# Chunked retention and a two-layer feed-forward on one core: a merged visit, a split last visit, held stores, and constants built by GpSimd

## The chip, the cores and the metric

The kernel runs on one core of one Trainium2 chip. The metric is the device time of one execution in microseconds (us). All times in this document are in us unless marked ns. The engines are called TensorE (PE in the profile, PEld for its weight loads), VectorE (DVE), ScalarE (ACT), GpSimd (POOL) and SyncE (SP); SPq and ACTq are the queues on which SP and ACT issue DMAs.

## The reference

Inputs q, k, v have shape (4, 8, 768, 64): 4 batches, 8 heads, 768 tokens, 64 features, float32. A decaying state runs over the tokens of each batch and head, and its output goes, heads joined, through two matrices with a leaky rectifier between them (w_in 512 x 2048, w_out 2048 x 512, alpha 2048).

```python
gamma = 1.0 - 2.0 ** (-5.0 - np.arange(H))
for t in range(S):
    state = gamma * state + outer(k[t], v[t])       # per batch and head, 64 x 64
    y[t] = q[t] @ state / sqrt(D)
x = y.transpose(0, 2, 1, 3).reshape(B * S, H * D)   # 3072 x 512
h = x @ w_in
out = (np.maximum(h, 0) + alpha * np.minimum(h, 0)) @ w_out   # 3072 x 512, float32
```

## The kernel before, in words

**Tiling.** The recurrence is computed in chunks. A unit u is 256 tokens of one batch (12 units); it has two windows w = 2u and 2u + 1 (24 windows). Up to window 7 a window is four heads of all 256 tokens, from window 8 on it is all heads of 128 tokens. Within a chunk the work is products of 64x64 tiles, four of which lie in PE's array at a time: scores (sc, keys with queries), a mask by DVE, products of the masked scores with v and of the queries with the carried state (both into y), and sums of keys with v for the next state. k and q are scaled beforehand by powers of gamma from a small table `tab` (kdq, by GpSimd or DVE), so the carried state tg needs a product with a power of gamma only now and then. ACT copies a finished y into xT, the input of the feed-forward.

The feed-forward works on blocks n = 0 to 5 of 512 tokens (two units each). `ffn1(n)` multiplies xT with w_in (hps), ACT makes the negative part (hm) and DVE joins both into gt; `ffn2(n)` multiplies gt with w_out (ops), ACT empties each finished bank into an os tile, and SP stores it. In `ffn2` each group of 128 tokens takes 16 products of 512 columns into one bank; block 0 takes three groups side by side (banks fa, fb, pa) and then the fourth (fa again).

**Order.** All order is written out by hand; each engine takes its instructions in the order of the program. `ffn1` and `ffn2` are generators, and `tick(gen, m)` lets m of their products go. Between ticks the program puts visits to the recurrence. A visit `both(u_old, u_new)` (L567 to L694) lets an old unit leave (products within the chunks L609, carries of state L587, ACT's copy to xT L660) and a new one enter (scores L632, sums L646, mask L669, states L681 to L687); either may be missing. The carries come in two halves, chunk equal to row half and unequal; the second half writes the same banks from the other row half and waits for `through(...)`, a tiny ACT instruction that tells that the first is done. Where no unit enters, three products of `gen` (`mid`, L622) fill that wait.

For n from 1 to 4 the loop at the end (L938 to L961) runs `ffn1(n)` and `ffn2(n)` with the visits for block n + 1, whose units are u0 = 2(n + 1) and u0 + 1: in block 1 `both(None, 4)`, `both(4, 5)`, `both(5, None)`; in block 2 `both(None, 6)`, `both(6, 7)`, `both(7, 8)`; later `both(u0, u0 + 1)` and `both(u0 + 1, u0 + 2)`, and in block 4 `both(11, None)` at the end. The first units go by functions of their own (`scores`, `within`, `finish`, `enter`, `pass_on`), with products of ones (`busy`) between them in the opening. `ahead()` scales the next window's k and q on GpSimd, has SP issue a DMA that transposes them into kq (`prep`, L233), and has SP load the window two further on (`load`, L169).

**Queues and buffers.** Nearly all DMAs are issued by SP, in the program's order: loads of q, k, v (L161, L169), of the weights in pieces (`fetch`, L192), the transposes and the stores (L797). q, k, v and the weight pieces share three rings of eight buffers (`ks`, `qs`, `vs`); stores have six of their own (`os`). A table `tab` (48 KB), a constant `mi` with mask and identity (128 KB) and alpha are loaded by ACT's queue first (L810 to L812).

Of the kernel before, what the change touches and what calls it, by code (L numbers as in the profile page):

```python
# [18 lines left out]
def kernel(  # L19
# [32 lines left out]
    pos = np.arange(128) % 64  # L52
    for a in range(2):
        for g in range(2):
            for x in range(2):
                for r in range(2):
                    h = 4 * g + 2 * r + x
                    col = 8 * g + 4 * r + 2 * x + a
                    tab_np[:, col] = g64[h] ** (127.0 - (2 * pos + a))
                    tab_np[:, 16 + col] = scale * g64[h] ** (2 * pos + a + 1.0 - 128.0)  # L60
    for g in range(2):
        for x in range(2):
            for r in range(2):
                tab_np[64 * r : 64 * r + 64, 32 + 2 * g + x] = g64[4 * g + 2 * r + x] ** 128
    for h in range(H):
        tab_np[:, 64 + h] = g64[h] ** (127.0 - np.arange(128))
        tab_np[:, 72 + h] = scale * g64[h] ** (np.arange(128) + 1.0 - 128.0)
# [3 lines left out]
    mi_np = np.zeros((128, 512), dtype=np.float16)  # L71
    for a in range(2):
        for b in range(2):
            mi_np[:, 128 * a + 64 * b : 128 * a + 64 * b + 64] = (2 * pos + a)[:, None] <= (
                2 * np.arange(64) + b
            )[None, :]
    mi_np[:, 256:384] = np.eye(128)
    mi_np[:, 384:448] = pos[:, None] <= np.arange(64)[None, :]

    tab_h = nc.inline_tensor(tab_np, name="tab_const")  # L80
    mi_h = nc.inline_tensor(mi_np, name="mi_const")
# [265 lines left out]
    def state(w, cs=None):  # L347
        u, g, b, c3 = place(w)
        decay = tab[:, 32 + 2 * g : 34 + 2 * g].unsqueeze(2).to_broadcast([128, 2, D])
        for c in cs or chunks(w):  # L350
            stv = sums.pop((w, c))[:, 0:128].rearrange("p (x e) -> p x e", e=D)
            gs = slice(2 * g, 2 * g + 2)
            if c3 + c > 0:
                nc.vector.tensor_tensor(out=stv, in0=tgs[2 * u + c][:, gs], in1=stv, op=ADD)
            to = 2 * u + c + 1 if 2 * u + c + 1 < NPE else 2 * NPE
            if to not in tgs:
                tgs[to] = new_state()
            nc.vector.tensor_tensor(out=tgs[to][:, gs], in0=stv, in1=decay, op=MULT)
# [130 lines left out]
    def all_state(key, cols):  # L489
        stv = cols.rearrange("p (z e) -> p z e", e=D)  # L490
        if key % (2 * NUS):
            nc.vector.tensor_tensor(out=stv, in0=tgs[key], in1=stv, op=ADD)
        to = key + 1 if key + 1 < NPE else 2 * NPE
        tgs[to] = new_state()
        nc.vector.tensor_tensor(
            out=tgs[to], in0=stv, in1=tab[:, 32:36].unsqueeze(2).to_broadcast([128, 4, D]), op=MULT
        )
# [69 lines left out]
    def both(u_old, u_new, mid=None):  # L567
# [11 lines left out]
        def carry(w, y, same, after=None):  # L579
            u, t, b, c3 = place(w)  # L580
            kq = live[w][1]
            for z in range(4):
                for r in range(2):
                    c = r if same else 1 - r
                    if c3 + 2 * t + c == 0:
# [5 lines left out]
                        start=False,  # L591
                        stop=True,
                        skip_group_check=True,
                    )
                    if after is not None:
# [4 lines left out]
        if old:  # L600
# [19 lines left out]
            done = through(last, nc.scalar)  # L620
            if not new:
                mid()  # L622
# [30 lines left out]
        if old:  # L653
            for w in old:
                carry(w, y, False, done if w == old[0] else None)
                live.pop(w)
            n, i = divmod(u_old, 2)
            if i == 0:
                xT[n] = new_x(n)
            nc.scalar.activation(  # L660
                out=xT[n][:, 4 * i : 4 * i + 4].rearrange("p s r (c i) -> p (s r) c i", c=2),
                in_=y.rearrange("p (c s i) -> p s c i", c=2, i=64),
                func=COPY,
                bias=0.0,
                scale=1.0,
            )
# [98 lines left out]
    def ffn2(n, groups=((0,), (1,), (2,), (3,)), tags="ffff", split=()):  # L765
# [3 lines left out]
        for tqs in groups:  # L769
# [3 lines left out]
            for at in parts:  # L773
                m = at.stop - at.start
                opss = {tq: ps("ops", tags[tq])[:, 0:m] for tq in tqs}
                for ft, tq in ((ft, tq) for ft in range(NFT) for tq in tqs):
# [7 lines left out]
                    if ft == NFT - 1:  # L784
                        row = TB * n + 128 * tq
                        for e in range(2 if at.start else 1):
                            cut = slice(e * m // 2, (e + 1) * m // 2) if at.start else slice(0, m)
                            os_sb = sbp.tile([128, d_model], FP, tag="os", bufs=6, name="os")
# [5 lines left out]
                            else:  # L794
                                nc.vector.tensor_copy(out=os_sb, in_=opss[tq][:, cut])  # L795
                            cols = slice(at.start + cut.start, at.start + cut.stop)
                            (nc.scalar if at.start and e == 0 else nc.sync).dma_start(  # L797
                                out=out[row : row + 128, cols], in_=os_sb
# [10 lines left out]
    nc.vector.memset(ones, 1.0)  # L809
    nc.scalar.dma_start(out=tab, in_=tab_h.ap())  # L810
    nc.scalar.dma_start(out=mi, in_=mi_h.ap())
# [67 lines left out]
    for i in range(4):  # L879
        if i == 1:  # L880
            load(5, "kq")
        for j in range(4):
            fetch("wo", i, j)
        if i < 2:
            load(4 + i, "v")
# [14 lines left out]
    gen = ffn2(0, ((0, 1, 2), (3,)), ("fa", "fb", "pa", "fa"))  # L900
# [7 lines left out]
    prep(7, opening=True)  # L908
# [29 lines left out]
    for n in range(1, NBLK):  # L938
# [9 lines left out]
        if n + 1 < NBLK:  # L948
            early = n < 3
# [3 lines left out]
            ahead()  # L953
            ahead()
# [3 lines left out]
            more_units = n > 1 and 2 * u0 + 4 < NW  # L958
            both(u0 + 1, u0 + 2 if more_units else None, lambda: tick(gen, 3))
# [32 lines left out]
```

## Time and profile before

| | before |
|---|---|
| time, median of 3 runs (lowest to highest) | 207.14 (206.74 to 207.25) |
| profiled execution, its own time | 205.89 |
| profiled execution, span from first to last instruction | 204.1 |
| granted TensorE clock, mean | 1.00 |
| PE / DVE / ACT / POOL busy | 197.7 / 122.0 / 98.0 / 76.7 |
| read from HBM, written to it | 27.45 MB, 6.29 MB |

The profile is of one execution. Its page gives busy times, the span in 40 slices, and the chain of work that ended last; the trace behind it answers with the chain piece by piece, the timeline of an engine, groups of instructions by line, and waits. L and a number is a line of the kernel before, except where a view of the kernel after is shown. A PE that is busy isn't a PE at its peak, and spans on POOL are rough.

### The profile page before, as it was taken

The page shows a single profiled execution, that of the slowest core. Times are in us where ns is not written, and L with a number is a line of the kernel's source. Part 1 is how long each engine was busy: PE and PEld are TensorE (multiplying, and loading weights), DVE is VectorE, ACT ScalarE, POOL GpSimd, SP SyncE. Part 2 cuts the span into 40 slices and gives each one's busy share as a digit, 9 for nine tenths or more (in the row PEclk, how much of TensorE's full clock was granted, in tenths as well). Part 3 has the DMA queues.
Part 4 walks back from the last instruction along what each step waited for, and adds up shares of the span by engine and source line. Part 5 has one row for each costly group of instructions (what it writes and reads, how often), then busy time and mean ns, then how long its engine had stood idle before and what let it go on. Part 6 is the DMA issues. An engine that isn't in the chain of part 4 may idle for free.

```text
span 204.1 us, 5640 instructions
## 1 busy us (share of the span) xinstructions
PE 197.7 (97%) x2343; PEld 104.4 (51%) x2343; DVE 122.0 (60%) x205; ACT 98.0 (48%) x166; POOL 76.7 (38%) x128
## 2 busy tenths in 40 slices
PE   7889999999999999999999999999999999999993
PEld 3567445557884454444455444545444544444462
DVE  2785886746799650588774688437588510688000
ACT  2585776056775133666133577313666313665121
POOL 0488985858805556455550055550000000000000
PEclk9999999999999999999999999999999999999999
DMA  6999999999999999999961499971510021100112
GB/s 180 340 369 345 353 366 392 384 302 224 295 218 241 223 211 222 309 200 233 237 188 57 116 218 221 223 206 56 132 24 0 3 106 51 51 0 3 51 65 89
DMA packets 88697, 38.30 MB, mean 188 GB/s; under 512 B 68304, under 2 KB 82144, under 8 KB 88672
## 3 DMA queue, kind: packets, MB, share of 16 engines
q1 hardware_dynamic: 88208, 37.69, 68.8%
q8 instruction: 18, 0.29, 0.6%
q10 hardware_dynamic: 464, 0.25, 0.4%
q14 instruction: 7, 0.06, 0.1%
HBM read 27.45 MB, written 6.29 MB: 165 GB/s over the span
## 4 chain that ended last, share of the span: by engine, by line
PE 91%; SPq 4%; DMA 3%; ACT 0%; issue 0%; POOL 0%; DVE 0%
PE ops L777 41%; PE hps L754 34%; PE hps L737 7%; SPq L161 4%; DMA vs<-in_v_dram 3%; PE y L609 1%; PE sc L632 1%; PE y L587 1%; PE sums L646 1%; PE trb L268 1%; PE y L395 1%; PE y L375 0%; ACT os L791 0%; PE sc L458 0%; SPq L192 0%
## 5 line engine op out<-in xcount | busy, mean ns | idle before, releaser
L699 DVE SCALAR_TENSOR_TENSOR gt<-hm,oma,hps 128x512 f16<-128x512 f32 (+1 forms) x112 | 73.3, 670 | 34.7 <-ACT hm L710 26.4
L777 PE MATMUL ops<-wout,gt 128*128 128x512 f16 (+1 forms) x400 | 87.0, 371 | 0.3 <-ACT os L791 0.3
L754 PE MATMUL hps<-xT,win 128*128 128x512 f16 x320 | 70.1, 379 | 0.0
L710 ACT ACTIVATE hm<-hps 128x512 f32<-128x512 f32 x96 | 57.2, 597 | 25.1 <-PE hps L754 21.3
L777 PEld LDWEIGHTS <-gt 128*128 128x128 f16 x400 | 37.9, 98 | 40.7 <-issue 0.5
L754 PEld LDWEIGHTS <-win 128*128 128x128 f16 x320 | 31.3, 98 | 37.5 <-DVE gt L699 0.4
L791 ACT ACTIVATE os<-ops 128x512 f32<-128x512 f32 (+2 forms) x25 | 14.2, 575 | 45.5 <-PE ops L777 45.5
L210 POOL TENSOR_TENSOR kdq<-ks,tab 128x256 f16<-128x256 f32 x32 | 18.9, 612 | 43.9 <-DMA ks<-in_k_dram 41.0
L669 DVE TENSOR_TENSOR m<-sc,mi 128x1024 f16<-128x1024 f32 x8 | 9.8, 1223 | 15.6 <-PE sc L632 15.6
L210 POOL TENSOR_TENSOR kdq<-qs,tab 128x256 f16<-128x256 f32 x32 | 18.9, 613 | 0.0
L737 PE MATMUL hps<-xT,win 128*128 128x256 f16 x128 | 15.2, 273 | 0.0
L737 PEld LDWEIGHTS <-win 128*128 128x128 f16 x128 | 12.0, 98 | 2.0
L409 ACT ACTIVATE word<-word 1x1 f32<-1x1 f32 x13 | 2.6, 201 | 18.2 <-PE y L587 16.4
L197 POOL CAST wout<-wo 128x512 f16<-128x512 f32 x16 | 10.1, 649 | 3.2 <-DMA wo<-in_moe_w_out_dram 3.0
L274 ACT ACTIVATE kq<-trb 128x512 f16<-128x512 f16 (+1 forms) x12 | 8.6, 736 | 4.2 <-PE trb L268 3.9
L660 ACT ACTIVATE xT<-y 128x1024 f16<-128x1024 f32 x8 | 8.2, 1024 | 4.6 <-PE y L587 4.6
L197 POOL CAST win<-wi 128x512 f16<-128x512 f32 x16 | 9.7, 613 | 0.9 <-DMA wi<-in_moe_w_in_dram 0.4
L240 POOL CAST vx<-vs 128x512 f16<-128x512 f32 x16 | 9.8, 610 | 0.7 <-DMA vs<-in_v_dram 0.4
L220 POOL TENSOR_TENSOR kdq<-qs,tab 128x512 f16<-128x512 f32 x5 | 5.2, 1042 | 9.7 <-DMA qs<-in_q_dram 9.7
L795 DVE COPY os<-ops 128x128 f32<-128x128 f32 x1 | 0.3, 292 | 12.8 <-ACT os L791 12.8
L248 PE MATMUL trb<-ones 128*128 128x512 f16 (+1 forms) x21 | 6.0, 408 | 1.5 <-DVE word L821 1.5
L268 PE MATMUL trb<-mi,kdq 128*128 128x128 f16 x64 | 5.6, 220 | 0.6 <-DVE kdq L220 0.4
(58 smaller groups left out, 112.3 us busy)
## 6 DMA issues: line engine op xcount, KB each, us to landing
ks<-in_k_dram SPq DMA_DIRECT2D x24, 256.0 KB, 4.1
qs<-in_q_dram SPq DMA_DIRECT2D x24, 256.0 KB, 4.4
vs<-in_v_dram SPq DMA_DIRECT2D x24, 256.0 KB, 4.6
out_dram<-os SPq DMA_DIRECT2D x23, 256.0 KB, 2.4
wi<-in_moe_w_in_dram SPq DMA_DIRECT2D x16, 256.0 KB, 5.4
wo<-in_moe_w_out_dram SPq DMA_DIRECT2D x16, 256.0 KB, 5.5
kq<-kdq SPq DMA_TRANSPOSE x16, 3.9
mi<-mi_const ACTq DMA_DIRECT2D x1, 128.0 KB, 3.1
```

The source lines that it names most:

```text
L197: nc.gpsimd.tensor_copy(out=dst, in_=t)
L210: eng.tensor_tensor(out=kdq[:, kind, 2 * i : 2 * i + 2].rearrange("p x r d -> p r x d"), in0=src[:, 2 * i : 2 * i + 2].rearrange("p r (x d ...
L240: nc.gpsimd.tensor_copy(out=vx, in_=v_in)
L274: nc.scalar.activation(out=kq.rearrange("p b i -> p (b i)")[:, cols], in_=trb[:, cols], func=COPY, bias=0.0, scale=1.0,)
L660: nc.scalar.activation(out=xT[n][:, 4 * i : 4 * i + 4].rearrange("p s r (c i) -> p (s r) c i", c=2), in_=y.rearrange("p (c s i) -> p s c i ...
L669: nc.vector.tensor_tensor(out=m2.rearrange("p (s i) -> p s i", i=64), in0=sc.rearrange("p (s i) -> p s i", i=64), in1=mask64.unsqueeze(1). ...
L699: nc.vector.scalar_tensor_tensor(out=gt[:, ft, lo : lo + hps.shape[1]], in0=hm, scalar=oma_sb[:, ft : ft + 1], in1=hps, op0=MULT, op1=ADD,)
L710: nc.scalar.activation(out=hm, in_=hps, func=RELU, bias=0.0, scale=-1.0)
L737: nc.tensor.matmul(out=bank[:, 256 * x : 256 * x + 256], lhsT=w_in_all[:, hp, 128 * ft : 128 * ft + 128], rhs=tokens[:, hp // 2, 2 * t : 2 ...
L754: nc.tensor.matmul(out=hps, lhsT=w_in_all[:, hp, 128 * ft : 128 * ft + 128], rhs=tokens[:, hp // 2, :, hp % 2, :], start=(hp == 0), stop=( ...
L777: nc.tensor.matmul(out=opss[tq], lhsT=gt[:, ft, 128 * tq : 128 * tq + 128], rhs=w_out_all[:, ft, at], start=(ft == 0), stop=(ft == NFT - 1),)
L791: nc.scalar.activation(out=os_sb, in_=opss[tq][:, cut], func=COPY, bias=0.0, scale=1.0)
```

## The change

Six things are done at once.

1. Blocks 2 and 3 share a visit: only block 1 has the early `both(None, u0)`. In block 1 the last visit becomes `both(5, 6)`, and in block 2 there are two visits, `both(6, 7)` after 14 products and `both(7, 8)` after 42.
2. The last unit leaves in one visit: `both(11, None)` writes the second half of the carries into a bank pair of its own (`y2`, tag s) with no wait and no products between; ACT copies two quarters of it out, DVE adds them to y, and ACT copies the two quarters of y that need nothing added.
3. Block 0's four stores are held: its os tiles lie in the rings of the loads, and SP issues the stores when window 14 has been loaded. `ahead(m)` now prepares m windows first and then loads, so that in `ffn2` the transposes of two windows stand before the loads.
4. Mask and identity are built by GpSimd (a memset and five `affine_select`); the load of `mi` is gone.
5. The tables are made for 256 tokens: the state is multiplied by a power of gamma once per unit, not once per chunk of 128, and merely copied or added in between, in the units before window 8 too.
6. In `ffn2` the last two products of each bank of a group stand together; window 7's k is scaled by GpSimd and its q by DVE (before the other way round); the load of window 5's v comes one weight piece earlier.

The diff, cut to its core:

```diff
     def state(w, cs=None):
-        decay = tab[:, 32 + 2 * g : 34 + 2 * g].unsqueeze(2).to_broadcast([128, 2, D])
+        decay = tab[:, 36 + 2 * g : 38 + 2 * g].unsqueeze(2).to_broadcast([128, 2, D])
...
+            if c3 + c == 0:
+                nc.vector.tensor_copy(out=tgs[to][:, gs], in_=stv)
+                continue
+            nc.vector.tensor_tensor(
+                out=stv if c else tgs[to][:, gs], in0=tgs[key][:, gs], in1=stv, op=ADD
+            )
+            if c:
+                nc.vector.tensor_tensor(out=tgs[to][:, gs], in0=stv, in1=decay, op=MULT)
...
-    def both(u_old, u_new, mid=None):
+    def both(u_old, u_new):
...
-            done = through(last, nc.scalar)
-            if not new:
-                mid()
+            if new:
+                done = through(last, nc.scalar)
+            else:
+                y2, done = ps("y2", "s"), None
...
         if old:
+            apart = set() if done is None else None
             for w in old:
-                carry(w, y, False, done if w == old[0] else None)
+                at = y2 if done is None else y
+                carry(w, at, False, done if w == old[0] else None, apart)
...
+                for c in range(2):
+                    part = sbp.tile([128, TB], FP, tag="hm", bufs=3, name="hm")[:, 0:256]
+                    part = part.rearrange("p (s i) -> p s i", i=64)
+                    nc.scalar.activation(
+                        out=part, in_=sums[:, :, 1 - c, c], func=COPY, bias=0.0, scale=1.0
+                    )
+                    nc.vector.tensor_tensor(
+                        out=to[:, :, 1 - c, c], in0=cells[:, :, 1 - c, c], in1=part, op=ADD
+                    )
+                for c in range(2):
+                    nc.scalar.activation(
+                        out=to[:, :, c, c], in_=cells[:, :, c, c], func=COPY, bias=0.0, scale=1.0
+                    )
...
-                for ft, tq in ((ft, tq) for ft in range(NFT) for tq in tqs):
+                steps = [(ft, tq) for ft in range(NFT - 2) for tq in tqs]
+                for ft, tq in steps + [(ft, tq) for tq in tqs for ft in (NFT - 2, NFT - 1)]:
...
+                                spare = "kqv"[len(held) % 3] + "s"
+                                os_sb = sbp.tile([128, 4, 2 * D], FP, tag=spare, bufs=8, name="os")
...
+                            if held is not None:
+                                held.append((to, os_sb))
+                                continue
...
+    nc.gpsimd.memset(ident, 0.0)
+    nc.gpsimd.affine_select(
+        out=ident,
+        in_=ident,
+        pattern=[[-1, 128]],
+        compare_op=mybir.AluOpType.not_equal,
+        fill=1.0,
+        base=0,
+        channel_multiplier=1,
+    )
+    for i in range(2):
+        rows = slice(64 * i, 64 * i + 64)
+        nc.gpsimd.affine_select(
+            out=mask[rows].rearrange("p (a b j) -> p a b j", a=2, b=2),
+            in_=ones[rows, 0:256].rearrange("p (a b j) -> p a b j", a=2, b=2),
...
+        nc.gpsimd.affine_select(
+            out=mask64[rows],
+            in_=ones[rows, 0:64],
...
-    nc.scalar.dma_start(out=mi, in_=mi_h.ap())
...
-    prep(7, opening=True)
+    prep(7, opening=True, k_on=nc.gpsimd, q_on=nc.vector)
...
-    def ahead():
-        w = more[0]
-        if w < NW:
+    def ahead(m=1):
+        ws = [w for w in range(more[0], more[0] + m) if w < NW]
+        for w in ws:
             prep(w)
+        for w in ws:
             if w + 2 < NW:
                 load(w + 2)
-            more[0] += 1
+            while w >= 12 and held:
+                to, src = held.pop(0)
+                nc.sync.dma_start(out=to, in_=src)
+        more[0] += m
...
-            early = n < 3
+            early = n == 1
             tick(gen, 2)
             if early:
                 both(None, u0)
-            ahead()
-            ahead()
+            ahead(2)
             tick(gen, 24 if early else 12)
             both(u0, u0 + 1)
             tick(gen, 26 if early else 28)
-            more_units = n > 1 and 2 * u0 + 4 < NW
-            both(u0 + 1, u0 + 2 if more_units else None, lambda: tick(gen, 3))
+            both(u0 + 1, u0 + 2 if 2 * u0 + 4 < NW else None)
```

More of the change, by code (lines that the diff above doesn't have):

```diff
@@ L577, in out_of, with carry @@
             return y[half(x), at : at + 64]
-        def carry(w, y, same, after=None):
+        def carry(w, y, same, after=None, started=None):
             u, t, b, c3 = place(w)
@@ L763, in ffn1, with ffn2 @@
                 yield
[L765 removed]
+    def ffn2(n, groups=((0,), (1,), (2,), (3,)), tags="ffff", split=(), held=None):
         gt = gts.pop(n)
```

91 lines of the change are left out of this document (56 added, 35 removed).

## The prediction

> **What bounds the kernel now.** I read the page first: the span, the engines' shares, the slices of the DMA engines.
>
> ```profile
> span 204.1 us, 5640 instructions
> ...
> PE 197.7 (97%) x2343; PEld 104.4 (51%) x2343; DVE 122.0 (60%) x205; ACT 98.0 (48%) x166; POOL 76.7 (38%) x128
> ...
> DMA  6999999999999999999961499971510021100112
> ```
>
> TensorE (PE) is busy 97% of the span. The DMA engines are nearly full through the first half, so a transfer can come late there. Next I read the chain that ended last in order of time (start, length, engine, what it writes), for the places where PE does something other than block products.
>
> ```profile
> 9.51 5.20 DMA vs<-in_v_dram
> ...
> 15.43 0.31 PE st L321 x8
> ...
> 42.75 0.61 ACT os L791
> ...
> 43.40 0.59 PE ops L777 x2
> ...
> 78.32 0.37 PE y L609 x32
> ...
> 79.83 2.05 PE ops L777 x9
> ...
> 96.13 0.38 PE sc L632 x32
> ...
> 96.84 5.29 PE ops L777 x24
> ...
> 109.07 0.38 PE y L609 x32
> ...
> 110.18 0.15 PE y L587 x16
> 110.33 2.70 PE ops L777 x12
> ...
> 167.44 0.38 PE y L609 x32
> ...
> 168.95 4.21 PE ops L777 x19
> 173.16 13.81 PE hps L754 x64
> ```
>
> Up to 15.43 the kernel waits for loads, last for v of window 3 (landed at 9.51 + 5.20 = 14.7). From there the chain is PE without a break, but for one stop before 43.40, while ACT empties a bank (42.75, 0.61 long, with 0.04 around it: 0.65). 64 full products take 13.81, so one costs 0.216 (the pitch). With PE full, an edit is worth what it takes out of PE's own sequence, out of that stop, or out of the opening.
>
> **The sum's base.** The profiled execution took 205.89, 1.79 more than its span, and lies 1.25 below the median of the three runs (207.14). I work out differences in the profiled execution and subtract them from the median. A measurement here can tell 0.3%, 0.62 us, from no change.
>
> **Blocks 2 and 3 share a visit.** Two visits go: the one in which unit 5 leaves alone, 79.83 - 78.32 less the three products inside it (3 x 0.216) = 0.86, and the one in which unit 6 enters alone, 96.84 - 96.13 = 0.71. One shared visit comes; such a one took 110.33 - 109.07 = 1.26. Gain 0.86 + 0.71 - 1.26 = 0.31, bounds 0.1 and 0.5 (an estimate, 0.2 each way: what a passage to another tile shape and back makes, 0.86 against 0.68 further down). DVE's masks and states only change place.
>
> That holds if unit 6 (windows 12 and 13) is ready some 18 us earlier than now. SP's queue and GpSimd's work, from the timeline, and the landing of transposes from the view of the tile kq:
>
> ```profile
> 51.89 2.13 SPq L797 DMA_DIRECT2D out_dram<-os  x3
> ...
> 60.27 0.85 SPq L797 DMA_DIRECT2D out_dram<-os  x1
> ...
> 70.54 1.75 SPq L233 DMA_TRANSPOSE kq<-kdq  x1
> ...
> 75.60 1.69 SPq L233 DMA_TRANSPOSE kq<-kdq  x1
> ...
> 86.69 2.65 SPq L233 DMA_TRANSPOSE kq<-kdq  x1
> ```
>
> ```profile
> 72.79 1.19 POOL L210 TENSOR_TENSOR kdq<-qs,tab 128x256 f16<-128x256 f32 x2
> ```
>
> ```profile
> DMA to landing us min/median/max: 2.7/3.9/6.0
> ```
>
> Counted in order, 70.54 and 75.60 are the transposes of windows 12 and 13. Left as it is, the second lands at 75.60 + 3.9 = 79.5, and the shared visit would read it at about 78.32 + 0.5 = 78.8: late. The held stores take 2.13 + 0.85 = 3.0 us of issue away ahead of it, and the transpose also passes window 14's three loads (72.3 to 75.6). What binds then is GpSimd's scaling of window 13, done at 72.79 + 1.19 = 74.0, and earlier by the same 3.0 as the loads it waits for: 71.0. Plus 3.9 the transpose lands at 74.9, at worst (6.0) at 77.0. PE, some 0.8 earlier by the gains below, reads it at 78.0. I cost the wait at nothing; the cover is 1 to 3 us, and each microsecond beyond it would be paid in full.
>
> SP now waits at window 13's transpose until 71.0. Behind it stand window 14's loads, the four held stores (3.0), then window 15's loads, which so come at their old time, at worst some 2 us later. Windows 14 and 15 were due at 96.84 + 5.29 = 102.1 and are now due near 99, as block 2's first visit moves forward by twelve products (2.6). Window 15's transpose was issued at 86.69: covered by 6 us or more. The held tiles take one or two of the eight places of each load buffer, and are given back before the ring comes round to them.
>
> **The last unit.** Its visit took 168.95 - 167.44 less three products = 0.86. It becomes its products 0.38 and two carries, the second into a bank of its own and without the way back to block products between them: 0.15 each (the carry of row 110.18) = 0.68. Gain 0.18, bounds 0 and 0.3. Off the path it adds copies; by the groups:
>
> ```profile
> L791 ACT ACTIVATE os<-ops 128x256 f32<-128x256 f32 x1 | 0.4, 384 | 1.1 <-PE ops L777 1.1
> ```
>
> Four copies of 256 columns (4 x 0.384 = 1.5) and two short DVE adds between them stand against the 22 products (4.7 us) that PE still has before the next block reads xT. That costs nothing; with the cover gone it would cost about 1.
>
> **The last two products of each bank together.** In block 0's group of three the first bank now ends four products before the group's end and not two, so ACT starts 2 x 0.216 = 0.43 earlier and PE's stop of 0.65 shrinks to an ordinary hand-over. Gain 0.42, bounds 0.25 and 0.5. Next late could be window 7's turn; its q was scaled here:
>
> ```profile
> 43.63 1.04 POOL L220 TENSOR_TENSOR kdq<-qs,tab 128x512 f16<-128x512 f32 x1 [2.39 <-DMA qs<-in_q_dram]
> ```
>
> ```profile
> L220 DVE TENSOR_TENSOR kdq<-qs,tab x3: 692/693/1099, 5.1 to 42.1; 128x512 f16<-128x512 f32 x3
> ```
>
> GpSimd ended at 44.67. PE came to it two products, a turn and four products after 43.40, about 45.1, and will come at 44.7. With the swap DVE scales q in 0.69: done at 44.3. No new wait. The v load of window 5 only passes one weight piece: 0.
>
> **The state's decay once per 256 tokens.** Some DVE products fall away in stretches where DVE waits for PE: 0.
>
> **Mask and identity by GpSimd.** A load of 128 KB goes from among the first ones (DMA issues; then one row of the stretches, whose last number is GB/s):
>
> ```profile
> mi<-mi_const ACTq DMA_DIRECT2D x1, 128.0 KB, 3.1
> ```
>
> ```profile
> 7.00:8.00 1.00, 1.00 (x23) 0.76 (x23) 0.67 (x2) 0.08 (x1) 0.71 (x1) 1.00 1.14 342
> ```
>
> 131 KB at 342 GB/s is 0.38, by which the loads behind it land earlier; the opening ends with such a load. Gain 0.35, bounds 0 and 0.4. Added are a memset and five selects on GpSimd. From the view of line 220, and the timeline:
>
> ```profile
> L220 POOLq MODIFY_POOL_CONFIG  x2: 11/11/11, 0.7 to 0.8; - x2
> ```
>
> ```profile
> 4.86 0.39 PE L268 MATMUL trb<-mi,kdq 128*128 128x128 f16 x4
> ...
> 7.29 1.04 POOL L220 TENSOR_TENSOR kdq<-qs,tab 128x512 f16<-128x512 f32 x1 [6.85 <-DMA qs<-in_q_dram]
> ...
> 7.42 1.23 DVE L336 TENSOR_TENSOR m<-sc,mi 128x1024 f16<-128x1024 f32 x1 [0.33 <-PE sc L296]
> ...
> 7.92 0.63 ACT L257 ACTIVATE vx<-vs 128x512 f16<-128x512 f32 x1 [1.01 <-DMA vs<-in_v_dram]
> ...
> 12.98 0.61 POOL L255 CAST vx<-vs 128x512 f16<-128x512 f32 x1
> ...
> 14.36 0.42 PE L296 MATMUL sc<-kq 64*64 64x128 f16 x16 [0.39 <-ACT kq L274]
> ```
>
> No select stands in this trace. The nearest row is GpSimd's cast, 0.61 for four times the columns: from 0.8 the identity is there by about 1.5 and the four masks at most 2.4 later. The first transposes run at 4.86 behind warming products, the mask is first read at 7.42: hidden. What the trace can't exclude is a silent preparation of GpSimd between MODIFY_POOL_CONFIG (0.8) and its first scaling (7.29), from 0 to 6.5 us, hidden so far behind the wait for qs. I take 0: the cast, an operation new at 12.98, started there without a gap. The other end is the first rival.
>
> **Sum.** 0.31 + 0.18 + 0.42 + 0.35 = 1.26, so 207.1 - 1.3 = 205.8; own range 205.4 to 206.3.
>
> **Rivals.** (1) GpSimd prepares silently before its first select. At the cap the identity comes at 7.29 + 0.61 = 7.9 and the first transposes go at 7.95, not 4.86, 3.1 later. Part is absorbed: 1.0 in ACT's wait for v (7.92), and some 0.4 at the end, where PE had its scores at 14.36 and could have gone on to the sums 0.6 later, not at 15.43. So transposes up to about 6.25 cost nothing, and at 7.95 the opening is 1.7 longer; against 0.91 won elsewhere the kernel takes 0.8 more: 207.9, slower. It is measurably slower from transposes at 7.8, and level from 6.5 on. For it: the first scaling stands behind that pair of MODIFY_POOL_CONFIG too, and no row shows what they cost. Against: that scaling started as soon as its load was there.
> The Trainium skill, GPSIMD Engine Reference, section 2.1 (Instruction dispatch), says that the first call to a freshly loaded kernel pays about 6 us (5.95 measured) which no instruction of a profile shows. By it the transposes go near 7.1 and the time is about 207.1 (estimate); this trace only caps it at 6.5.
> (2) Window 13's transpose doesn't come earlier, since the DMA engines, full in those slices, and not the order of issue set its time. It lands at 79.5, the visit reads it at 78.0 and stalls 1.5, and 1.26 - 1.5 leaves 207.4. Against: the stores leave the DMA engines as well.
> (3) The loads of the opening don't move, and the smaller gains come at their lower bounds: 0.25 + 0.1 = 0.35, 206.8.
>
> **Chances.** Forecast 0.56; rival 1 0.32, half of it early enough to end level and half slower; rival 2 0.06, split evenly; rival 3 0.06, level. So faster 0.56, level 0.16 + 0.03 + 0.06 = 0.25, slower 0.19. The range, 205.3 to 207.9, takes in rivals 2 and 3 and rival 1 to its cap; left out are a preparation that holds up the masks too, and gains above their bounds.
>
> **What would show it.** GpSimd's selects should stand before 4 us, the first transposes at 4.86, and the sums of window 3 near 15.1. If the transposes start after 6.3 right behind the selects, rival 1 holds. PE's stop before 43.40 should be gone. A visit of y, sc, sums and y should stand near 77, 1.3 long, with no wait ahead of sc (rival 2: a wait there for a DMA); near 166 y and its two carries in one piece. The prediction is wrong if the stretch from the sums of window 3 (15.43) to the last block's first products (173.16), 157.7 long now, doesn't shrink by 0.6 to 1.2.

## The result, and the profile after

The changed kernel took 205.31 (median of 6 runs, 205.15 to 205.52), the kernel before in the same comparison 207.55 (6 runs, 206.74 to 208.16). The ratio is 0.9893, 95% interval 0.9867 to 0.9919. Two later comparisons, 12 runs of the changed kernel each, gave 0.9940 (0.9914 to 0.9966) and 0.9931 (0.9896 to 0.9965). The forecast, 205.8 after 207.14, is a ratio of 0.9935: the two later comparisons lie on it, the first shows more, and its 205.31 is just below the prediction's own range of 205.4 to 206.3. Runs over 1.5% above the fastest of their kernel are left out of a ratio, and so of this table of all comparisons together (10 of the 121 of before, none of the 30 of after):

| | before | after | distance |
|---|---|---|---|
| tenth percentile | 206.01 | 205.04 | 0.97 |
| median | 207.09 | 205.43 | 1.66 (interval 1.31 to 1.96) |
| ninetieth percentile | 208.08 | 206.51 | 1.57 |

So the shortest executions lie about 1.0 apart, less than the forecast 1.26, and the middle and longer ones about 1.6. The two profiled executions lie only 0.37 apart (205.89 and 205.52). From the page of the changed kernel, in the order of the lines shown of before, with the shares of the chain below them:

```profile
span 203.5 us, 5647 instructions
...
PE 197.9 (97%) x2343; PEld 105.2 (52%) x2343; DVE 121.6 (60%) x204; ACT 98.1 (48%) x168; POOL 78.1 (38%) x134
...
DMA  5999899999899979999998499961510021100112
...
PE 96%; DVE 1%; ACT 1%; issue 0%; DVEq 0%
```

PE is as full as before. In the first half the DMA engines have a few slices of 7 and 8 among the nines. The chain runs through PE almost from the start. The chain in order of time (start, length, engine, what it writes):

```profile
5.75 0.43 PE trb L238
...
15.86 0.12 PE st L311 x8
...
37.02 6.80 PE ops L804 x31
...
46.08 0.57 PE y L391 x32
...
78.22 0.38 PE y L613 x32
78.59 0.13 PE y L589 x15
78.72 0.32 PE sc L637 x31
79.04 0.29 PE sums L651 x32
79.34 0.16 PE y L589 x15
79.49 2.70 PE ops L804 x12
...
112.61 13.81 PE hps L779 x64
...
142.87 13.81 PE hps L779 x64
...
167.03 0.38 PE y L613 x32
167.40 0.26 PE y L589 x30
167.67 4.86 PE ops L804 x22
172.52 13.81 PE hps L779 x64
```

Block 0's products now go through from 37.02 to 43.82 with no stop. The shared visit is one piece from 78.22 to 79.49, 1.27 long. The last unit is one piece from 167.03 to 167.67, 0.64 long. To cut the time into stretches, three rows of the same view of the kernel before are needed beside those of the prediction:

```profile
46.18 0.57 PE y L395 x32
...
113.03 13.81 PE hps L754 x64
...
143.28 13.81 PE hps L754 x64
```

| stretch | before | after | gain | forecast |
|---|---|---|---|---|
| start to the end of window 3's sums (15.43 + 0.31, 15.86 + 0.12) | 15.74 | 15.98 | -0.24 | 0.35 |
| to y at 46 (block 0, the stop) | 30.44 | 30.10 | 0.34 | 0.42 |
| to hps at 113 (blocks 1 and 2, the visits) | 66.85 | 66.53 | 0.32 | 0.31 |
| to hps at 143 (block 3) | 30.25 | 30.26 | 0 | 0 |
| to hps at 173 (block 4, the last unit) | 29.88 | 29.65 | 0.23 | 0.18 |

What PE was to save it saved, 0.89 where 0.91 was forecast; two later profiles of the changed kernel give 1.01 and 0.95 by the same stretches. The opening didn't get shorter. GpSimd's timeline in the changed kernel, where the selects stand:

```profile
0.80 0.20 POOL L846 MEMSET mi<- 128x128 f16 x1 [0.29 <-POOLq L1046]
1.08 0.29 POOL L847 TENSOR_SCALAR_AFFINE_SELECT mi<-mi 128x128 f16<-128x128 f16 x1
1.53 0.42 POOL L858 TENSOR_SCALAR_AFFINE_SELECT mi<-ones 64x256 f16<-64x256 f16 x1 [0.16 <-DVE word L886]
1.91 0.23 POOL L867 TENSOR_SCALAR_AFFINE_SELECT mi<-ones 64x64 f16<-64x64 f16 x1
2.20 0.42 POOL L858 TENSOR_SCALAR_AFFINE_SELECT mi<-ones 64x256 f16<-64x256 f16 x1
2.58 0.24 POOL L867 TENSOR_SCALAR_AFFINE_SELECT mi<-ones 64x64 f16<-64x64 f16 x1
```

All is built by 2.82, and no gap stands ahead of the first select.

### The profile page after: what moved, and what is told of

Its sections match the earlier page's. It is cut to its first block, busy times and chain, and to the rows that moved or that the text cites. A ratio compares the mean times of both kernels' runs of the same rounds, so it can differ in the third digit from the quotient of the medians.

```text
span 203.5 us, 5647 instructions
## 1 busy us (share of the span) xinstructions
PE 197.9 (97%) x2343; PEld 105.2 (52%) x2343; DVE 121.6 (60%) x204; ACT 98.1 (48%) x168; POOL 78.1 (38%) x134
## 4 chain that ended last, share of the span: by engine, by line
PE 96%; DVE 1%; ACT 1%; issue 0%; DVEq 0%
PE ops L804 41%; PE hps L779 34%; PE hps L762 7%; PE trb L238 3%; PE trb L258 2%; PE y L613 1%; PE sc L637 1%; PE y L391 1%; PE sums L651 1%; PE y L589 1%; PE sc L238 1%; PE y L371 1%; DVE m L326 1%; ACT kq L264 1%; PE sc L286 1%; PE sc L454 0%
## 5 line engine op out<-in xcount | busy, mean ns | idle before, releaser
L669 ACT ACTIVATE xT<-y 128x1024 f16<-128x1024 f32 x7 | 7.2, 1023 | 3.8 <-PE y L589 3.8
L238 PE MATMUL trb<-ones 128*128 128x512 f16 (+1 forms) x21 | 6.5, 435 | 1.6 <-DVE word L886 1.5
L258 PE MATMUL trb<-mi,kdq 128*128 128x128 f16 x64 | 6.1, 231 | 0.0
L706 DVE TENSOR_TENSOR sums<-tg,sums 128x256 f32<-128x256 f16 x13 | 5.6, 429 | 0.8
```

The lines of the kernel that those rows point to most:

```text
L238: nc.tensor.matmul(out=at[:, 0:n], lhsT=ones[:, 0:128], rhs=ones[:, 0:n], start=True, stop=True)
L258: nc.tensor.transpose(out=trb[:, 128 * i : 128 * i + 128], in_=flat[:, 128 * i : 128 * i + 128], identity=ident,)
```

## The experiments

Two accounts of the excess were set against each other. By the first, the moment at which PE's clock becomes full differs from execution to execution and lengthens the opening; by the second, late transfers do, in the opening and in the stretch in which the DMA engines are full, and the change removes load there or adds cover. Every kernel ran beside the kernel before on one chip. One reading serves all of them, so it comes first: in each profile the end of window 3's sums, and the rest of the span behind it.

| kernel | sums of window 3 end | rest of the span (good to 0.05, since spans are printed to 0.1) |
|---|---|---|
| before, its first profile | 15.74 | 188.36 |
| before, a second profile | 16.37 | 188.33 |
| before with built constants | 15.79 | 188.41 |
| before with shared visit and held stores | 16.61 | 188.09 |
| before with the unit leaving in one visit | 16.09 | 188.51 |
| before with the last two products together | 15.91 | 188.29 |
| before with v of window 5 earlier and the swap | 16.99 | 188.71 |
| changed, three profiles | 15.98, 16.09, 16.19 | 187.52, 187.41, 187.51 |
| changed, constant loaded again | 15.55 | 187.45 |
| changed, stores not held | 16.05 | 187.35 |
| changed, idle load of 256 KB | 17.98 | 187.22 |
| changed, shorter warm-up | 15.70 | 187.80 |

The rest is nearly the same in the two executions of before and in the three of the changed kernel, and 0.8 to 0.95 shorter after the change. The opening moves from one execution to another: between 15.55 and 16.99 in the seven profiles with the constant loaded, between 15.70 and 16.19 in the six with it built and no idle load. On average the six are 0.2 earlier, which is less than the spread of either.

What moves it can be read off one load. In twelve of the fourteen profiles the sums end 1.03 after v of window 3 landed (14.71 and 15.74 in the first profile of before). In the other two, the unit leaving in one visit and the first of the changed kernel, that v landed early, at 13.82, and PE's own products behind window 3's k end the opening, at 16.09 and 15.98.

### The kernel before again

No edit.

> The kernel before, unchanged, as one more sample: its profiled execution took 205.89, its timed ones up to 208.16. Theory 1 (the granted clock): PE's clock goes to full at another moment of the opening in each execution (4.64 in the profile before), and the time of the kernel before follows that moment; a profile with a later moment then shows the opening longer by 1 to 2 us and the rest, 157.7 from the sums of window 3 to the last block's first products, unchanged. Theory 2 (a late transfer): in most executions PE waits for a transfer later on, and the rest is longer than 157.7 by 1 to 2.

It took 207.33 (12 runs, 205.82 to 209.42), 1.0007 (0.9971 to 1.0043) of the kernel before. Its chain:

```profile
7.13 4.55 DMA ks<-in_k_dram
...
11.75 1.05 POOL kdq L220
...
12.84 0.40 PE trb L268 x4
...
16.01 0.06 PE y L375 x4
16.07 0.30 PE st L321 x8
```

Here the sums of window 3 stand behind other PE work and not behind a load as at 15.43, but that work goes back to a load: k of window 3 landed at 11.68, where the first profile has 10.93, GpSimd scaled it, and PE's transposes of it began at 12.84, where the first has 12.10. v of window 3 landed 0.63 later too, at 15.34. The later opening (0.63) is the whole difference between the two spans, 204.7 and 204.1; the rest is equal. The trace records the full clock from 7.47 on, against 4.64 in the first profile, but PE waits for the scaled k after that, so the clock isn't what made this opening longer. Theory 1 is right that the opening moves and the rest stays; its cause is not borne out, its 1 to 2 were 0.6, and neither theory explains runs of 208 and above.

### The constants alone

```diff
-    nc.scalar.dma_start(out=mi, in_=mi_h.ap())
+    nc.gpsimd.memset(ident, 0.0)
+    nc.gpsimd.affine_select(out=ident, in_=ident, ...
...
```

> The kernel before with mask and identity built by GpSimd and no load of mi, nothing else. The prediction gave it -0.35 (0 to -0.4). Theory 1: the opening's gain depends on the clock, and this part can carry the 0.9 by which the timed gain (2.2) exceeds the forecast (1.3): then -1 or more. Theory 2: -0.35, since the rest isn't touched.

206.05 (12 runs, 205.60 to 207.31), ratio 0.9965 (0.9935 to 0.9995): 0.72 faster, interval 0.10 to 1.35. That lies between the two values expected, and the interval holds both. The clock became full at 7.44, as late as in the kernel before's second profile, and the sums ended 0.58 earlier than there (15.79 and 16.37), as v of window 3 landed 0.59 earlier (14.75 and 15.34). The rest of the span, 188.41, is that of the kernel before.

### The shared visit with held stores alone

```diff
-            early = n < 3
+            early = n == 1
...
-            more_units = n > 1 and 2 * u0 + 4 < NW
+            more_units = 2 * u0 + 4 < NW
...
+    gen = ffn2(0, ((0, 1, 2), (3,)), ("fa", "fb", "pa", "fa"), held=held)
```

> The kernel before with the shared visit of blocks 2 and 3, the held stores and two windows' transposes ahead of the loads, nothing else. The prediction gave -0.31 (0.1 to 0.5). Theory 2: the held stores take a late transfer out of most executions, and this part carries the excess: about -1.2. Theory 1: -0.3.

206.54 (12 runs, 205.87 to 207.85), ratio 0.9994 (0.9961 to 1.0028). By time alone it can't be told from the kernel before (0.12 faster, interval -0.58 to 0.81), and Theory 2's 1.2 is excluded. By the trace the rest is 0.2 to 0.3 shorter, although in this execution PE waited for the v of window 5, issued at 30.34 and landed 6.56 later, at 36.90. That wait took 0.26: from the sums' end to the 27 products of block 0 it is 21.30, against 21.04 in both profiles of before. The stretch of blocks 1 and 2, in which the visits lie, took 66.34, where before has 66.85 and 66.83: 0.5 less, at the upper bound of the forecast 0.31.

### The leave in one visit alone

The edit takes in both units that leave alone in the kernel before, 5 and 11; in the changed kernel it is unit 11 alone.

```diff
-            done = through(last, nc.scalar)
-            if not new:
-                mid()
+            if new:
+                done = through(last, nc.scalar)
+            else:
+                y2, done = ps("y2", "s"), None
```

> The kernel before with the one-visit leave (second carries into a bank of their own, the sum by ACT and DVE) at both places where a unit leaves alone, units 5 and 11, nothing else. The prediction gave 0.18 for one, so -0.36 for both by theory 1 and by theory 2; 0 if the carries cost as much as the way back and forth.

206.64 (12 runs, 205.40 to 209.28), ratio 0.9976 (0.9945 to 1.0006). Its chain, and the one row of PE's timeline near 46 that has a wait:

```profile
38.89 6.30 DMA qs<-in_q_dram
...
45.27 1.05 POOL kdq L220
...
144.00 13.81 PE hps L777 x64
...
173.66 13.81 PE hps L777 x64
```

```profile
46.37 0.40 PE L268 MATMUL trb<-mi,kdq 128*128 128x128 f16 x4 [0.29 <-POOL kdq L220]
```

Block 4 takes 29.66, as in the changed kernel, where the kernel before has 29.88: 0.22 for the last unit. The stretch from y at 47.19 to hps at 113.75, in which unit 5 leaves, takes 66.56, 0.29 less than before. The rest as a whole is no shorter, because q of window 7 landed late, GpSimd's scaling of it came late, and PE stopped for 0.29 at window 7's turn; with smaller delays ahead of that stop, the stretch from the sums to that y took 31.10, 0.66 more than before. The prediction had named that scaling as the next thing to be late; here it was, and the kernel had neither the swap nor the load moved.

### The last two products of a bank together, alone

```diff
-                for ft, tq in ((ft, tq) for ft in range(NFT) for tq in tqs):
+                steps = [(ft, tq) for ft in range(NFT - 2) for tq in tqs]
+                for ft, tq in steps + [(ft, tq) for tq in tqs for ft in (NFT - 2, NFT - 1)]:
```

> The kernel before, with only the last two products of each bank put together. By the prediction 0.42 faster (bounds 0.25 and 0.5), with no PE stop near 43 in the profile. The rival: window 7's q (scaled by GpSimd here, ended at 44.67 in the profile before) comes next and gives back what the hand-over gained: 0 to 0.1 faster, and a wait of PE at window 7's turn.

206.11 (12 runs, 205.47 to 208.19), ratio 0.9973 (0.9943 to 1.0004). The chain:

```profile
30.65 5.56 DMA vs<-in_v_dram
...
37.22 6.80 PE ops L778 x31
...
45.58 0.40 PE trb L268 x4
```

```profile
44.47 1.04 POOL L220 TENSOR_TENSOR kdq<-qs,tab 128x512 f16<-128x512 f32 x1 [2.43 <-DMA qs<-in_q_dram]
```

The stop near 43 is gone: the 31 products are one piece of 6.80, as in the changed kernel. From 37.22 to the y at 46.40 it takes 9.18; the kernel before took 9.40 (36.78 to 46.18). So 0.22 of the 0.42 is left there. The other 0.20 went at window 7's turn, where the rival had it: GpSimd ended the scaling of its q at 45.51, and the turn took from 45.33 to 45.97, 0.64, where before took 0.45. Ahead of the 31 products PE also waited for v of window 5, landed at 36.21, and the rest of the span is no shorter than before's by more than 0.07.

### The two small moves alone

```diff
+            if (i, j) == (1, 3):
+                load(5, "v")
...
-    prep(7, opening=True)
+    prep(7, opening=True, k_on=nc.gpsimd, q_on=nc.vector)
```

> The kernel before, with only window 5's v loaded one weight piece earlier and window 7's k and q swapped between GpSimd and DVE. The prediction gave both 0. Theory A1 (late v of window 5 and late q of window 7 are what lengthens the kernel before): median 0.5 to 1 below the kernel before, its slow executions gone. Theory A2 (the opening's phase of the clock and the 128 KB load are it): within 0.3 of the kernel before.

207.16 (12 runs, 205.96 to 210.21), ratio 0.9994 (0.9967 to 1.0020). Theory A1 is wrong: the two moves alone do nothing for the time, and the long executions stay. The profiled execution was itself a long one, 207.51, so its profile shows where such time goes. Its chain, then its rows of SP's queue and of PE:

```profile
16.01 0.63 POOL vx L255
...
16.68 0.31 PE st L321 x8
...
68.75 4.54 DMA kq<-kdq
```

```profile
54.32 1.90 SPq L797 DMA_DIRECT2D out_dram<-os  x3
...
63.27 0.82 SPq L797 DMA_DIRECT2D out_dram<-os  x1
...
68.75 2.54 SPq L233 DMA_TRANSPOSE kq<-kdq  x1
```

```profile
73.34 0.32 PE L632 MATMUL sc<-kq 64*64 64x64 f16 x16 [0.19 <-DMA kq<-kdq]
```

First, v of window 3 landed at 15.96, 1.25 later than in the first profile of before; GpSimd cast it from 16.01 on, and the sums end at 16.99. Second, the transpose of window 11, behind all four stores in SP's queue, landed at 73.29, and PE, which had come to its scores, stopped (the rest of the span is 188.71, 0.35 above before's). Call cover the time by which a transfer has landed ahead of the products that read it. By the landings in the trace, the cover of that transpose ahead of the sixteen scores that read it was 0.86, 0.38, 0.27, 0.23 and 0.20 in the profiles of before and of its variants with stores at once that had no stop there.

### The changed kernel twice more

No edit.

> The changed kernel again, as the mark for this group of runs. Medians so far: 205.3 for it, 206.9 to 207.6 for the kernel before, while the two profiled executions differ by 0.37 only. Theory A (the change also takes away late loads that lengthen many executions of the kernel before): the times stay within 0.5 of 205.3, and the fastest execution of the kernel before is within 0.8 of the fastest of this one although the medians lie 1.5 to 2.2 apart. Theory B (the same gain in every execution): the fastest ones lie as far apart as the medians.

> The changed kernel once more, as the mark for this group: a median of 205.2 to 205.6, and the transpose of window 11 landing 0.7 to 4 ahead of the scores that read it, where the kernel before and its variants with stores not held showed 0.2 to 0.8, and one of them a stop of 0.4.

205.36 (12 runs, 204.86 to 207.09) and 205.61 (12 runs, 205.10 to 207.50). The fastest runs beside them, 205.69 and 205.60 for the kernel before, are 0.83 and 0.50 above its fastest, while the medians lie 1.73 and 1.59 apart. That speaks for Theory A, that part of the gain is not in every execution, though not wholly: single executions of the changed kernel reached 207.09 and 207.50, and 0.83 is just over its 0.8. That late loads are this part is not shown by it. The cover of window 11's transpose was 0.76, 3.12 and 2.67 in the three profiles.

### The changed kernel with the constant loaded again

```diff
-    nc.gpsimd.memset(ident, 0.0)
-    nc.gpsimd.affine_select(out=ident, in_=ident, ...
...
+    nc.scalar.dma_start(out=mi, in_=mi_h.ap())
```

> The changed kernel with the 128 KB constant loaded again and nothing built by GpSimd. By the prediction 0.35 slower than the changed kernel. Theory A2: 0.6 to 1.1 slower in the median, with slow executions above 206.5 back. Theory A1: 0.3 to 0.5 slower and as narrow as the changed kernel.

206.50 (12 runs, 204.78 to 209.54), ratio 0.9967 (0.9933 to 1.0000) to the kernel before; the changed kernel beside it had 0.9940. That is 0.56 slower by the ratios, whose intervals overlap, and 1.06 by the medians (interval 0.13 to 1.53 against the 30 runs). Executions above 206.5 became more frequent, as Theory A2 has it: five, besides the one at 209.54, where the changed kernel has three of thirty. Yet the fastest of its runs, 204.78, is as fast as any of the changed kernel, and was the profiled one, with the shortest opening of all:

```profile
15.24 0.31 PE st L321 x8
```

So the load does not lengthen every opening. It makes long executions more frequent; in which part of them the time goes was not profiled.

### The changed kernel with block 0's stores issued at once

```diff
-    gen = ffn2(0, ((0, 1, 2), (3,)), ("fa", "fb", "pa", "fa"), held=held)
+    gen = ffn2(0, ((0, 1, 2), (3,)), ("fa", "fb", "pa", "fa"))
```

> The changed kernel with block 0's stores issued at once. The prediction's account (3.0 of SP's issue ahead of windows 12 and 13): window 13's transpose comes some 3 later than the 76.7 of the changed kernel, 79.7, against a need at 78.7, so the shared visit waits about 1, and window 11's cover shrinks by as much: 0.5 to 1.5 slower than the changed kernel. The rival (the loads' landing and not SP's order sets these times): no wait before the shared visit's scores, within 0.2 of the changed kernel.

206.24 (12 runs, 204.85 to 207.36), ratio 0.9942 (0.9910 to 0.9975), where the changed kernel beside it had 0.9931: by the ratios 0.2 slower, by the medians 0.64 (interval -0.09 to 1.14) against that one and 0.82 (0.28 to 1.24) against the 30 runs. Its rows of SP's queue, and the scores of the shared visit on PE:

```profile
65.28 2.44 SPq L223 DMA_TRANSPOSE kq<-kdq  x1
...
71.19 5.02 SPq L223 DMA_TRANSPOSE kq<-kdq  x2
```

```profile
78.45 0.49 PE L637 MATMUL sc<-kq 64*64 64x64 f16 x32
```

The prediction's account of the held stores is wrong for window 13. Its transpose landed at 77.45 without them being held, 0.8 later than in the changed kernel and not 3.0, and the scores show no wait. What brings it forward is that `ahead(2)` issues the transposes of windows 12 and 13 one behind the other (the row at 71.19), ahead of window 14's loads: the second was issued at 74.55, right behind GpSimd's scaling (done at 74.52), where the kernel before has 75.60 for a scaling done at 73.98. What holding the stores does may be seen at window 11: landed at 71.38 for scores at 71.63, a cover of 0.25.

### An idle load at the place of the one that went

```diff
+    extra = sbp.tile([128, 1024], F16, tag="extra", name="extra")
+    nc.scalar.dma_start(out=extra, in_=extra_h.ap())
```

> The changed kernel with an idle load of 256 KB, read by nobody, at the place of the 128 KB that went: it delays the loads behind it and holds up no instruction. If the traffic of the first loads sets the opening: 0.77 later by the rate of 342 GB/s, so 0.5 to 0.9 slower than the changed kernel, and the first sums of window 3 at 16.3 or later. If it was the wait of transposes and masks for the constant that mattered, or nothing of it: within 0.2 of the changed kernel.

205.83 (12 runs, 205.03 to 207.61), ratio 0.9939 (0.9904 to 0.9974); against the changed kernel beside it 0.22 by the medians, interval -0.42 to 1.22. The 0.5 to 0.9 expected is neither seen nor excluded. The profiled execution had a very late opening:

```profile
10.51 6.44 DMA vs<-in_v_dram
...
17.67 0.31 PE st L312 x8
```

v of window 3 landed at 16.95, where the three profiles of the changed kernel have 13.82 to 15.16, and the sums ended at 17.98. That is more than 0.77, in one execution, and the other runs did not show it on average. How much of the constant's price is traffic, and how much the wait for the constant itself, stays open.

### A shorter warm-up

```diff
-    turn(0, "f", (0,), fill=34)
+    turn(0, "f", (0,), fill=30)
...
-    scores(0, fill=10)
+    scores(0, fill=8)
```

> The changed kernel with 30 in place of 34 products of ones ahead of the first transposes (one of 512 columns less) and 8 in place of 10 ahead of the first scores. If the opening is bound by PE in the executions whose clock is granted late (after 7): 0.1 to 0.4 less in those, 0.1 to 0.2 in the median. If loads bound it in most executions: no change. If PE's idle time in the opening keeps the clock at half for one more window of 3.4: slower by up to 1.7 in some executions.

205.61 (10 runs, 205.04 to 206.37), ratio 0.9916 (0.9884 to 0.9947), the median equal to that of the changed kernel beside it. The profiled opening ended at 15.70, with the clock full at 6.72; the later part of that span was 0.3 to 0.4 longer, as PE waited for DVE's scaling ahead of the transposes at 34.24. No version was found that is measurably faster than the changed kernel.

## Why the prediction was right, and where it was not

**The bound and the base.** PE's own sequence sets the time from the opening on: right, the rest of the span repeats within 0.15 and falls by what is taken out of the sequence. Subtracting from the median is right only in part. The tenth percentile moved by 0.97, the median by 1.66: the sum leaves out what differs from execution to execution, which one profile of before, itself 1.25 below the median, does not show. Late transfers fit it (the long profile above has two), but how much of the median is theirs stays open; by the ratios the five parts alone gave 0.72, 0.12, 0.50, 0.56 and 0.12, each with an interval of 0.6 or 0.7 either way, so none carries it by itself. That the two later comparisons, 1.24 and 1.43, meet the 1.26 is in part luck, since 0.35 of it is a term whose working failed.

**Shared visit, 0.31.** Measured 0.32 (0.37 and 0.30 in the later profiles); the new visit is 1.27 long where 1.26 was forecast. No wait: window 13's transpose, issued at 73.94, landed at 76.67, and the scores read it at 78.72. The place was right and the reason wrong. The step that failed is that the 3.0 of the stores would bring window 13's loads, and with them GpSimd's scaling, forward from 74.0 to 71.0. The scaling was done at 73.92 in the changed kernel (73.04 and 73.61 in the later profiles):

```profile
72.73 1.19 POOL L200 TENSOR_TENSOR kdq<-qs,tab 128x256 f16<-128x256 f32 x2
```

What the transpose gained, 75.60 to 73.94, comes with the order of transposes and loads: it now goes right behind the scaling, and not behind window 14's loads. Why window 13's loads did not come earlier is open. That the cover of 2.05 lies within the forecast 1 to 3 is luck: the landing took 2.7 and not 3.9, and PE came at 78.7 and not at 78.0. Further on, window 15's transpose was issued at 90.68, 4.0 later than before, and landed 4.6 ahead of its scores, not 6 or more. Whatever the held stores are worth would be at window 11, which the prediction did not look at, and whose cover before was under 1; but the kernel before with shared visit and held stores had a cover of 3.85 there and was not measurably faster.

**Last unit, 0.18.** Measured 0.22 and 0.23. Its visit is 0.64 and not 0.68, as both carries go in one piece of 0.26. The copies stay off the path, as costed; here are their rows on ACT (DVE's two adds stand between, at 168.15, 0.76 long together), done by 169.6, with PE's products lasting to 172.52:

```profile
167.73 0.66 ACT L682 ACTIVATE hm<-y 128x256 f32<-128x256 f32 x2 [2.23 <-PE y L589]
...
168.94 0.66 ACT L689 ACTIVATE xT<-y 128x256 f16<-128x256 f32 x2 [0.55 <-DVE xT L685]
```

**Last two products together, 0.42.** Measured 0.34 in the first profile and 0.42 in the other two of the changed kernel. Window 7's q is scaled by DVE, and PE's turn at 44.96 began without a wait:

```profile
44.31 0.88 DVE L210 TENSOR_TENSOR kdq<-qs,tab 128x512 f16<-128x512 f32 x1 [0.76 <-DMA qs<-in_q_dram]
```

It ended at 45.19 and not at 44.3, since q itself landed only at 44.29 and the scaling took 0.88 and not 0.69; the second half of the turn waited 0.08 for it, which is the difference between 0.34 and 0.42. Without the swap, the kernel with the leave alone stopped 0.3 for the same q, and the one with the last two products together lost 0.20. So the swap is worth something in executions with a late q, and the two small moves alone gave no difference in the median, 0 as forecast.

**Mask and identity, 0.35.** The term whose working failed. It took the opening to end with a load, so that each load behind the 128 KB would bring the end forward. It does end 1.03 after v of window 3 in twelve profiles; but the landing of that v differs from execution to execution by more than 0.38. In the first profile after it came at 13.82 and not at 14.71, in the other two at 15.06 and 15.16. And when it comes early, another path binds: k of window 3 landed at 10.87, only 0.06 earlier than before, PE went on to its transposes at 12.12, and its products behind them end at 15.98, among them a pause of 0.22 before y at 15.61 for which the profile shows no cause. The late clock (full at 7.12 and not at 4.64; the product of ones at 5.75 takes 0.43, twice the pitch of 0.216) can have cost 0.15 there at most, since the scaled k was ready at 11.97. The average over executions is another thing than these profiles: the constants alone gave 0.72 (0.10 to 1.35), and taking them back cost 0.56 by the ratios. The first interval holds the 0.35, both estimates lie above its bound of 0.4, and the size stays uncertain.

**Decay of the state, 0.** It was not tried alone. The stretch of block 3, where nothing else changed, took 30.25 and 30.26.

**The rivals.** The first, a silent preparation of GpSimd, is wrong: memset, selects and all stand before 2.82, and the first transposes at 5.12 come behind PE's own products. The Trainium skill, GPSIMD Engine Reference, section 2.1 (Instruction dispatch), has a first call pay about 6 us that no instruction of a profile shows; here the first select begins at 1.08, 0.08 after the memset ends, so for this operation the trace shows no such time, and the measurement decides; whether its code was freshly loaded, the trace doesn't tell. The second, a late transpose of window 13, is wrong in every profile of the changed kernel and even with the stores at once. Of the third, that the opening doesn't move is what the profile shows and the average doesn't; that the other gains come at their lower bounds is wrong.

**The test it set itself.** From the sums' start to the last block's first products 157.7 was to shrink by 0.6 to 1.2. By the chain's starts (15.86 to 172.52) it shrank by 1.07, by the ends of the sums by 0.88. Of the signs named, the sums near 15.1 did not come (15.86); the stop gone, the visit of 1.3 and the last unit in one piece did.

## What to carry to other kernels

Where one engine runs in one piece, a sum of what is taken out of its sequence comes out to a tenth of a microsecond here, and a place to look for the rest is the cover of each transfer, counted over all of them and not only at the place of the edit. A transfer whose cover is under 1 us in one profile can be late in another execution, as at window 11 here; what it is worth in the median, to take stores out of its queue or to issue it ahead of loads, was not shown. A cause that fits the clock should be followed back along the chain before it is believed: here it led to a load. Two profiles of the same kernel, set side by side at one fixed instruction, tell what belongs to the execution and what to the kernel.

## What the runs showed of the hardware

The moment at which PE's clock became full lay between 4.64 and 7.47 in the fourteen profiles, with PE busy from 1.45 to 1.52 on. From there the record shows a full clock for 197.97, and for 201.39 in two of them: 58 and 59 times 3.413. The clock is thus granted by windows of 3.413 that do not start with the kernel. The window from 1.23 to 4.64, in which PE was busy 93% of the time, was enough to make it full; those from 0.30 to 3.71 and from 0.65 to 4.06, 64% and 76% busy, were not. The Trainium skill, TensorE: Matmul & The Clock Gate, Part 1, gives that window of 3413 ns, running free of the kernel's start, and the trace agrees; it has the moment vary by 0.5 us either way, and here it spread over 2.8. What this costs the kernel is at most 0.3 as far as the profiles tell: in the two whose opening did not end with window 3's v, PE reached the transposes of window 3's k 0.15 and 0.27 after GpSimd had scaled it.

A clock that falls later on is another matter. Of the kernel before, 115 executions have their mean granted clock on record; 23 took 207.98 or more, and 12 of these show 0.989 or 0.992, as none of the shorter ones does. 0.008 of 206 is 1.65, close to what one window of 3.413 at half the clock takes away (1.71, an estimate). None of them was profiled, so what let the clock fall is open. Of the 30 of the changed kernel one shows 0.989, at 207.36.

The five selects took 0.23 to 0.42 each, for 64 to 256 columns. A transfer is done when the last of the DMA engines is (in the long profile the first was done at 73.15, the last at 73.29, and PE's scores started at 73.34): window 11's transpose landed within 0.4 from the first to the last engine in twelve profiles, but took 1.7 in two, where covers of 0.86 and 0.76 were left.
